# Four loads of v with four consecutive rows per partition, and token order restored as the TensorE transpose is evacuated

## The chip, the cores and the metric

The kernel runs on one core of one Trainium2 chip. The metric is the device time of one execution in microseconds (us). The engines are PE (TensorE, matrix multiply), DVE (VectorE), ACT (ScalarE) and POOL (GpSimd, which here mainly issues DMA transfers). This kernel's matmuls write their tiles to PSUM; "evacuating" a tile is copying it from there to SBUF, where the next operations of the kernel read it. Times printed by the profiler are counted from the start of the span, and the span is 1.7 to 1.9 us shorter than the device time of the same run.

## The reference

```python
# q, k, v: (4, 6208, 256) f32; 256 channels, 6208 tokens
qn = q / (norm(q, axis=tokens) + 1e-6);  kn likewise
a  = softmax(kn^T @ qn / tau)             # 256 x 256 for each batch
x  = v @ a                                # 6208 x 256
x_prev = x shifted down by one token
xk = mu_k * x + (1 - mu_k) * x_prev       # xr likewise, with mu_r
k  = relu(xk @ w_k);  out = sigmoid(xr @ w_r) * (k * k @ w_v)
```

The shift by one token matters here: the kernel keeps x transposed, channels on partitions and tokens along the free dimension, and takes the difference of neighbouring columns. So v, transposed, must stand in token order.

## The kernel before

First come the covariance q^T k of batch 0 and its softmax (0 to 41 us). Then a pipeline over 48 blocks of 512 tokens and one of the 256 left over: v is transposed, x = v a, mix with the previous token, up (w_k), square, down (w_v). Blocks 0 to 3 are transposed by PE, because they are needed soon; the other full blocks by the DMA engines. The parts that the change touches:

```python
P = 128; M = 512; S = 4                      # partitions, tokens per block, M // P

def v_load(i):
    v_bf = p2.tile([P, S, C], BF16, ...)
    nc.gpsimd.dma_start(v_bf, v[b, t*M:(t+1)*M, :].rearrange("(s p) c -> p s c", p=P))

def v_transpose_pe(i, evac):                 # blocks 0 to 3
    vT_ps = ps.tile([P, S, 2, P], BF16, ...)
    for s in range(S):
        for h in range(2):
            nc.tensor.transpose(vT_ps[:, s, h], v_bf[:, s, h*P:(h+1)*P], ident)
    if i == 0:
        return lambda: evac(vT0[:, :, 1:].rearrange("c h (s p) -> c s h p", s=S), vT_ps)
    vT = p2.tile([P, S, 2, P], BF16, ...)
    return lambda: evac(vT, vT_ps)
```

and the places where they are used (cuts marked with dots):

```python
    v_load(1); <load w_k, 512 KB>; ...; v_load(2); <load w_v>; v_load(3); ...
    go = v_transpose_pe(0, nc.vector.tensor_copy)   # block 0: evacuated by DVE
    ...; go(); ...; difference(0); exp()
    v_transpose_pe(1, nc.scalar.copy)()             # block 1: by ACT
    keep_warm(2)                                    # two junk matmuls of 512 columns
    weigh_first(0); weigh_first(1); difference(1)   # a_sb, the weights of the softmax
    ... product(a, ih) ...                          # x of block 0 (x_ps)
    # in the loop over blocks:
            if (i, j) in ((-1, 6), (0, 4)):
                v_transpose_pe(i + 3, nc.vector.tensor_copy)()   # blocks 2 and 3: by DVE
```

## Time and profile before

Three runs gave 511.42 to 511.74 us, median 511.45. The profiled run took 512.12 us, with a span of 510.2.

| Reading | Value | View |
|---|---|---|
| PE, DVE, ACT busy | 95%, 87%, 87% of the span | the page, part 1 |
| PE waits for block 1 of v | 1.5 us, once | waits, by PE |
| PE waits for block 2's copy | 0.8 us, once | waits, by PE |
| Copies 128x1024 PSUM to SBUF | 0.67 to 0.68 us on DVE, 1.01 on ACT | timeline |
| PE clock 39.8 to 43.2 us | 0.50 of the full one | windows |

Two lines of the page, the span and the busy times in us with their share and the number of instructions:

```profile
span 510.2 us, 9336 instructions
...
PE 485.9 (95%) x3441; PEld 331.3 (65%) x3441; DVE 444.0 (87%) x751; ACT 446.3 (87%) x925; POOL 99.9 (20%) x146
```

The waits of PE, who waited for whom, then us in total, times, and the longest:

```profile
PE vT_ps L365 <- DMA v_bf<-in_v_dram: 1.5, 1, 1.5
...
PE xT_ps L386 <- DVE vT L371: 0.8, 1, 0.8
```

The timeline at the places that the argument uses; columns are start, duration, engine, line, operation, output<-input, shapes, and in brackets the idle time before and what ended it:

```profile
38.52 0.67 DVE L368 COPY vT<-vT_ps 128x1024 bf16<-128x1024 bf16 x1
...
40.39 1.04 PE L365 MATMUL vT_ps<-ident,v_bf 128*128 128x128 bf16 x8 [1.50 <-DMA v_bf<-in_v_dram]
...
42.08 0.63 PE L410 MATMUL x_ps<-vT,a_sb 128*128 128x256 bf16 x2
...
48.53 0.69 DVE L469 TENSOR_TENSOR delta<-xT 128x1024 bf16<-128x1024 bf16 x1 [1.11 <-ACT xT L388]
...
52.20 0.68 DVE L371 COPY vT<-vT_ps 128x1024 bf16<-128x1024 bf16 x1
...
52.94 0.59 PE L386 MATMUL xT_ps<-vT,a_sb 128*128 128x512 bf16 x2 [0.83 <-DVE vT L371]
```

The first line is block 0's copy, the second block 1's transposes, waiting for their load. Then come the first matmul of x for block 0, the first "delta" of the loop (the token difference of block 1), block 2's copy, and the x matmul that waits for it. The load of block 1, asked for alone (the line of the load, in the window of that one issue):

```profile
L349 POOL DMA_DIRECT2D v_bf<-in_v_dram x1: 940/940/940, 33.3 to 33.3; - x1
...
DMA to landing us min/median/max: 7.1/7.1/7.1
```

POOL worked 940 ns at it from 33.3 us, and the data had landed 7.1 us after the start, at 40.4. The windows view, of which the columns needed are the stretch, its length, the busy times of PE, PEld, DVE, ACT and POOL, then the granted PE clock, the DMA share and GB/s:

```profile
39.00:40.00 1.00, 0.00 (x0) 0.00 (x0) 0.93 (x6) 1.00 (x5) 0.16 (x1) 0.88 1.13 199
...
41.00:42.00 1.00, 1.00 (x7) 0.53 (x5) 0.05 (x1) 0.53 (x1) 0.46 (x1) 0.50 1.14 213
...
45.00:46.00 1.00, 0.67 (x5) 0.26 (x4) 1.00 (x3) 0.66 (x2) 0.48 (x2) 1.00 1.45 195
```

In the middle one PE runs at half its clock (0.50 granted). The DMA queues then move 2 KB packets (w_k) at 213 GB/s; in the last one they move 512-byte packets at 195 GB/s.

### The profile page before, as it was taken

The numbers are of one execution on the slowest core, as the hardware profiler recorded it, in microseconds if no ns is written. First come the engines' busy times: TensorE is split into PE (matmuls) and PEld (weight loads), VectorE is DVE, ScalarE is ACT, GpSimd is POOL, SyncE is SP. The second block draws the span as 40 slices with busy tenths as digits, with TensorE's granted clock in tenths as the row PEclk, the third lists the DMA queues.
The fourth block names the chain that finished last, engine by engine and source line by source line (L and its number), as shares of the span: only waits on it lengthen the run. The fifth ranks groups of instructions, "written<-read, shape, count | busy, mean of one in ns | idle before, by whom it ended". The sixth has DMA issues, their size and how long they took to land. (4 is left out here: it accounts for less than half of the span.)

```text
span 510.2 us, 9336 instructions
## 1 busy us (share of the span) xinstructions
PE 485.9 (95%) x3441; PEld 331.3 (65%) x3441; DVE 444.0 (87%) x751; ACT 446.3 (87%) x925; POOL 99.9 (20%) x146
## 2 busy tenths in 40 slices
PE   4678999999999999999999999999999999999996
PEld 1345666766567677676666767667666666666675
DVE  3776899999999999999979999999878787878884
ACT  5767999999899999999899999999897888888784
POOL 0044342223054132221243133000131100000000
PEclk9998999999999999999999999999999999999999
DMA  8999999999989999997599999924497763333123
GB/s 330 409 299 201 191 173 199 143 192 199 201 153 198 180 205 172 171 184 134 102 157 227 173 173 177 176 74 116 84 178 137 143 106 97 93 85 83 45 81 104
DMA packets 133462, 83.46 MB, mean 164 GB/s; under 512 B 50660, under 2 KB 126760, under 8 KB 133416
## 3 DMA queue, kind: packets, MB, share of 16 engines
q0 software_dynamic: 56592, 33.01, 50.1%
q1 hardware_dynamic: 76504, 49.59, 41.1%
q8 instruction: 27, 0.44, 0.4%
q10 hardware_dynamic: 320, 0.26, 0.2%
q14 instruction: 19, 0.16, 0.1%
HBM read 78.71 MB, written 25.43 MB: 204 GB/s over the span
## 5 line engine op out<-in xcount | busy, mean ns | idle before, releaser
L499 ACT ACTIVATE kr<-kT_ps 128x512 bf16<-128x512 f32 (+1 forms) x390 | 232.0, 606 | 27.8 <-PE kT_ps L494 24.0
L531 PE MATMUL vr_ps<-w_v_sb,kk 128*128 128x256 bf16 x1536 | 231.0, 273 | 0.1
L494 PE MATMUL kT_ps<-xk,w_k_sb 128*128 128x512 bf16 (+1 forms) x780 | 230.0, 377 | 0.2 <-DVE xk L479 0.2
L531 PEld LDWEIGHTS <-kk 128*128 128x128 bf16 x1536 | 149.5, 98 | 58.9 <-DVE kk L512 1.1
L541 DVE SCALAR_TENSOR_TENSOR res<-res,vr_ps 128x256 f32<-128x256 f32 x192 | 80.1, 417 | 42.8 <-ACT res L540 42.8
L512 DVE TENSOR_TENSOR kk<-kr 128x1536 bf16<-128x1536 bf16 (+2 forms) x148 | 117.1, 791 | 0.2 <-ACT kr L499 0.2
L494 PEld LDWEIGHTS <-w_k_sb 128*128 128x128 bf16 x780 | 75.5, 98 | 27.5 <-issue 0.6
L230 DVE TENSOR_TENSOR acc<-acc,sq 128x1024 f32<-128x1024 f32 x69 | 84.2, 1220 | 0.0
L540 ACT ACTIVATE res<-vr_ps 128x256 f32<-128x256 f32 x192 | 76.5, 398 | 1.3 <-PE vr_ps L531 1.3
L527 PE MATMUL vr_ps<-w_r_sb,xr 128*128 128x256 bf16 x384 | 73.3, 272 | 1.2 <-DVE res L541 1.2
L479 DVE SCALAR_TENSOR_TENSOR xr<-delta,mu_t,xT 128x512 bf16<-128x512 bf16 x94 | 70.1, 746 | 0.0
L479 DVE SCALAR_TENSOR_TENSOR xk<-delta,mu_t,xT 128x512 bf16<-128x512 bf16 x94 | 70.1, 746 | 0.0
L527 PEld LDWEIGHTS <-xr 128*128 128x128 bf16 x384 | 37.6, 98 | 46.4 <-issue 2.6
L388 ACT CAST xT<-xT_ps 128x512 bf16<-128x512 f32 x94 | 55.4, 589 | 12.1 <-PE xT_ps L386 11.9
L386 PE MATMUL xT_ps<-vT,a_sb 128*128 128x512 bf16 x188 | 55.9, 379 | 0.9 <-DVE vT L371 0.8
L242 PE MATMUL s_ps<-qk 128*128 128x256 bf16 (+1 forms) x294 | 55.8, 273 | 0.0
L127 POOL DMA_DIRECT2D qk<-in_q_dram x39 | 26.2, 672 | 136.6 <-ACT kr L499 53.3
L226 ACT ACTIVATE sq<-qk 128x1024 f32<-128x1024 bf16 (+1 forms) x49 | 51.0, 1041 | 0.0
L349 POOL DMA_DIRECT2D v_bf<-in_v_dram x48 | 37.1, 776 | 50.7 <-DMA vT<-v_bf 32.4
L190 PE MATMUL s_ps<-qk 128*128 128x384 bf16 (+2 forms) x98 | 20.3, 352 | 16.0 <-ACT qk L147 14.9
L469 DVE TENSOR_TENSOR delta<-xT 128x1024 bf16<-128x1024 bf16 x47 | 32.3, 686 | 1.1 <-ACT xT L388 1.1
L242 PEld LDWEIGHTS <-qk 128*128 128x128 bf16 (+1 forms) x294 | 28.5, 98 | 5.6 <-issue 0.8
(105 smaller groups left out, 242.1 us busy)
## 6 DMA issues: line engine op xcount, KB each, us to landing
out_dram<-res SPq DMA_DIRECT2D x47, 512.0 KB, 4.2
v_bf<-in_v_dram POOLq DMA_DIRECT2D x48, 256.0 KB, 9.0
qk<-in_q_dram POOLq DMA_DIRECT2D x36, 256.0 KB, 8.0
qk<-in_k_dram POOLq DMA_DIRECT2D x36, 256.0 KB, 8.8
f<-in_q_dram SPq DMA_DIRECT2D x11, 512.0 KB, 9.4
f<-in_k_dram SPq DMA_DIRECT2D x11, 512.0 KB, 9.9
vT<-v_bf SPq DMA_TRANSPOSE x44, 6.7
f<-in_q_dram SPq DMA_DIRECT2D x2, 256.0 KB, 9.0
```

The costliest lines, as they stand in the source:

```text
L230: nc.vector.tensor_tensor(sums[b], sums[b], t, op=OP.add)
L242: nc.tensor.matmul(s_ps[:, ih, :], rows_at(qk, b, g, 0)[:rows, s, ih * P:(ih + 1) * P], rows_at(qk, b, g, 1)[:rows, s, :], start=t0 and ih ...
L386: nc.tensor.matmul(xT_ps, a_sb[:, b, ih, dh * P:(dh + 1) * P], vT[:, :, ih, :], start=ih == 0, stop=ih == 1)
L388: nc.scalar.copy(xT[:, dh, 1:], xT_ps)
L479: nc.vector.scalar_tensor_tensor(o[:, dh], st[i, "d"][:, dh], mu[:, dh:dh + 1], st[i, "x"][:, dh, :M], op0=OP.mult, op1=OP.add)
L494: nc.tensor.matmul(kT_ps[:, :m], w_k_sb[:, dh, fh * P:(fh + 1) * P], xk[:, dh, :m], start=dh == 0, stop=dh == 1)
L499: nc.scalar.activation(kr, kT_ps[:, :m], AF.Relu, scale=0.5 ** 0.5)
L512: nc.vector.tensor_tensor(st[i, "kk"][:, fh // 4 * 4 + lo:fh + 1, :m], kr, kr, op=OP.mult)
L527: nc.tensor.matmul(vr_ps[:, D:], xr[:, dh, s * P:(s + 1) * P], w_r_sb[:, dh, :], start=dh == 0, stop=dh == 1)
L531: nc.tensor.matmul(vr_ps[:, :D], kk[:, fh, s * P:(s + 1) * P], w_v_sb[:, fh, :], start=fh == 0, stop=fh == 7)
L540: nc.scalar.activation(res[:, s], vr_ps[:, D:], AF.Tanh, scale=0.5)
L541: nc.vector.scalar_tensor_tensor(res[:, s], res[:, s], 1.0, vr_ps[:, :D], op0=OP.add, op1=OP.mult)
```

## The change

The intent: a load that gives each partition four consecutive rows reads 128 runs of 4 KB instead of 512 of 1 KB. That is a quarter of the packets (the run with the change has 131,926 for 133,462, so 384 fewer for each of the four loads) and less work on POOL (548 ns for the load of block 1, against 940). The transposed tile then has its tokens out of order, and since the kernel copies it out of PSUM anyway, the copy can put them in order for nothing, if a stepped source costs nothing.

```diff
     def v_load(i):
-        nc.gpsimd.dma_start(v_bf, v[b, t * M:(t + 1) * M, :].rearrange("(s p) c -> p s c", p=P))
+        nc.gpsimd.dma_start(v_bf, v[b, t * M:(t + 1) * M, :].rearrange(
+            "(p s) c -> p s c" if i < S else "(s p) c -> p s c", p=P))
     def v_transpose_pe(i, evac):
         ...
+        src = vT_ps.rearrange("c s h p -> c h p s")
         if i == 0:
-            return lambda: evac(vT0[:, :, 1:].rearrange("c h (s p) -> c s h p", s=S), vT_ps)
-        vT = p2.tile([P, S, 2, P], BF16, name="vT", tag="vT", bufs=5)
-        st[i, "vT"] = vT
-        return lambda: evac(vT, vT_ps)
+            vT = vT0[:, :, 1:]
+        else:
+            vT = p2.tile([P, S, 2, P], BF16, ...).rearrange("c s h p -> c (s h p)")
+            st[i, "vT"] = vT.rearrange("c (h s p) -> c s h p", h=2, s=S)
+            vT = vT.rearrange("c (h m) -> c h m", h=2)
+        return lambda: evac(vT.rearrange("c h (p s) -> c h p s", s=S), src)
```

The copy writes densely; its source now steps 256 elements (512 bytes) from one element to the next, in groups of four. Below, "the new load" is the first part and "the stepped copy" the second.

More of the change, by code (lines that the diff above doesn't have):

```diff
@@ L365, in v_transpose_pe @@
                 nc.tensor.transpose(vT_ps[:, s, h], v_bf[:, s, h * P:(h + 1) * P], ident)
+        src = vT_ps.rearrange("c s h p -> c h p s")
         if i == 0:
-            return lambda: evac(vT0[:, :, 1:].rearrange("c h (s p) -> c s h p", s=S), vT_ps)
-        vT = p2.tile([P, S, 2, P], BF16, name="vT", tag="vT", bufs=5)
-        st[i, "vT"] = vT
-        return lambda: evac(vT, vT_ps)
+            vT = vT0[:, :, 1:]
+        else:
+            vT = p2.tile([P, S, 2, P], BF16, name="vT", tag="vT", bufs=5).rearrange("c s h p -> c (s h p)")
+            st[i, "vT"] = vT.rearrange("c (h s p) -> c s h p", h=2, s=S)
+            vT = vT.rearrange("c (h m) -> c h m", h=2)
+        return lambda: evac(vT.rearrange("c h (p s) -> c h p s", s=S), src)
     def x_half(i, dh):
```

## The prediction

> **What bounds the kernel.** The page shows PE busy 485.9 of 510.2 us (95%), DVE and ACT 87%; the chain that ended last runs through PE matmuls, so after the start a delay of PE is a delay of the end. In the table of windows PE is idle 15 us in 0 to 31 us (the first covariance, fed by DMA) and busy 10.0 of 10 us in 60 to 70. The change touches only 32 to 60 us.
>
> **What changes.** Four of 48 loads of v: same bytes, but 128 runs of 4 KB (f32) instead of 512 of 1 KB. Costs, from the trace:
>
> - Descriptors on POOL: v loads 742 to 940 ns each; the q/k loads of the second batch, already of the new shape, 531 to 591. About 0.25 us less per load.
> - Packets: 512 of 512 B (60 ns each) become 128 of 2 KB (173 ns each). In steady stretches these queues move 195 and 213 GB/s, so a load takes 1.33 and 1.23 us of the queue: 0.1 us saved[...].
> - Evacuation: the source now steps 512 B between neighbouring elements. The DVE copies of 128x1024 take 0.67 to 0.68 us[...]. I expect [...]as the 128x1024 f32 add has (1.22 us): 1.2 us, 0.54 more, for blocks 0, 2 and 3. Block 1's copy is on ACT (1.01 us) and should stay near 1.0.
> - PE work is unchanged; the written tile is dense.
>
> **What is on the critical path.**
>
> 1. Gain. PE waits 1.5 us for v of block 1 (waits by PE: "DMA v_bf", once), until 40.39; the load was issued at 33.3 and landed after 7.1 us[...]. Transposes, two warming matmuls, then the x products (42.08), ACT (43.47) and DVE (43.88) follow. With earlier issue and fewer packets I expect landing at 39.4 to 40.0. DVE then nearly binds: its copy of block 0 (38.52) pushes the softmax weights from 40.71 to about 41.25 and the second difference to 41.6, so products can start near 41.3. Gain 0.4 to 0.9 us, perhaps 1.5 if the half clock (39.8 to 43.2 us, granted 0.5) is avoided.
> 2. Loss. PE waits for block 2's copy (52.20 to 52.88; wait 0.83 us, "DVE vT", until 52.94), and DVE has no gap from 48.5 on. The extra 0.54 us goes straight to PE, which has almost no idle time later.
> 3. Block 3's copy (59.45, used at 62.7) has 2.6 us of slack and DVE idles 0.55 us at 68.3: nearly free.
>
> Sum: about -0.6 + 0.54, near zero.
>
> **Prediction.** 511.3 us, 8 times in 10 between 510.3 and 512.3. Faster by over 2%: 1%; within 2%: 98%; slower by over 2%: 1%.
>
> **What would show each step.** POOL v loads 0 to 3 at 0.55 to 0.6 us; some 1,500 packets fewer; DVE vT copies at 1.2 us, the ACT copy at 1.0; PE's wait for v_bf under 1.5 us, x products before 42.08; from the first product to block 2's x matmul, 10.86 us before, about 11.4; from 60 us on the same schedule, shifted.
>
> **What would make it wrong.** A strided PSUM read [...] (2 us or more): slower by 1 to 3 us. Block 1 landing no earlier, because other traffic[...] sets it: about 512.0. The PE clock staying full around 40 us: about 510. Shifted loads colliding later: some tenths either way.

The terms of its sum, -0.6 for block 1 and +0.54 for block 2's copy, come to -0.06 us from 511.45, and the prediction put its middle at 511.3. The 0.54 is the 1.22 us of the f32 add less 0.68; that a stepped bf16 copy would take as long as that add was the author's estimate, not shown before the run. The landing at 39.4 to 40.0 us is an estimate; of what the text gives for it, POOL's 0.25 us and the queue's 0.1 us remain, so most of the 0.4 to 0.9 us of gain is that estimate.

## The result, and the profile after

Ratios here are the mean time of one kernel's fast runs over that of the other's of the same rounds, so they are not quite the ratios of the medians quoted beside them.

The first measurement: 510.56 us median (510.54 to 510.63, 4 runs), before 511.44 (510.46 to 511.74, 4 runs), ratio 0.9986, 95% interval 0.9969 to 1.0004. That is the same within 2%, and 0.3 us above the lower end of the predicted range, 510.3 to 512.3. The lines of the changed kernel that answer to those shown of before, first the page:

```profile
span 508.8 us, 9277 instructions
...
PE 481.0 (95%) x3382; PEld 330.3 (65%) x3441; DVE 445.2 (88%) x751; ACT 446.1 (88%) x925; POOL 99.2 (20%) x146
```

(The 59 PE records fewer are missing from the trace, not from the program: the weight loads, one for each matmul, are 3441 in both.) The waits of PE:

```profile
PE xT_ps L390 <- DVE vT L375: 1.4, 1, 1.4
...
PE x_ps L414 <- DVE a_sb L328: 0.7, 1, 0.7
```

The timeline at the same places:

```profile
38.32 1.20 DVE L375 COPY vT<-vT_ps 128x1024 bf16<-128x1024 bf16 x1
...
38.38 0.61 PE L366 MATMUL vT_ps<-ident,v_bf 128*128 128x128 bf16 x8
...
39.86 1.01 ACT L375 COPY vT<-vT_ps 128x1024 bf16<-128x1024 bf16 x1
...
40.64 0.39 PE L414 MATMUL x_ps<-vT,a_sb 128*128 128x256 bf16 x2 [0.69 <-DVE a_sb L328]
...
46.59 0.69 DVE L473 TENSOR_TENSOR delta<-xT 128x1024 bf16<-128x1024 bf16 x1 [1.11 <-ACT xT L392]
...
50.26 1.22 DVE L375 COPY vT<-vT_ps 128x1024 bf16<-128x1024 bf16 x1
...
51.53 0.59 PE L390 MATMUL xT_ps<-vT,a_sb 128*128 128x512 bf16 x2 [1.36 <-DVE vT L375]
```

The load of block 1, asked for alone, landed at 33.1 + 5.2 = 38.3 us:

```profile
L349 POOL DMA_DIRECT2D v_bf<-in_v_dram x1: 548/548/548, 33.1 to 33.1; - x1
...
DMA to landing us min/median/max: 5.2/5.2/5.2
```

The window from 41 to 42 us of the changed kernel, now at full clock:

```profile
41.00:42.00 1.00, 1.00 (x12) 0.80 (x10) 0.44 (x3) 0.47 (x2) 0.01 (x1) 1.00 1.17 219
```

These two traces tell a neat story. The load landed at 38.3 instead of 40.4 us. The x products started 1.44 us earlier (40.64 against 42.08), now held by DVE's weights. The half clock was gone, and the first delta came 1.94 us earlier (46.59 against 48.53). The stepped copy of block 2 took 0.54 us longer, and PE waited 1.36 instead of 0.83 us for it, so 1.41 us were left at the x matmul (51.53 against 52.94) and at the end (508.8 against 510.2). The experiments show that the last third of this story is right, and that most of the first two thirds is what these two executions happened to draw.

### The profile page after: what moved, and what is told of

It reads as the page before. It is cut to its first block, busy times and chain, and to the rows that moved or that the text cites. A ratio compares the mean times of both kernels' runs of the same rounds, so it can differ in the third digit from the quotient of the medians.

```text
span 508.8 us, 9277 instructions
## 1 busy us (share of the span) xinstructions
PE 481.0 (95%) x3382; PEld 330.3 (65%) x3441; DVE 445.2 (88%) x751; ACT 446.1 (88%) x925; POOL 99.2 (20%) x146
## 2 busy tenths in 40 slices
DMA packets 131926, 83.46 MB, mean 164 GB/s; under 512 B 50660, under 2 KB 124712, under 8 KB 131880
## 5 line engine op out<-in xcount | busy, mean ns | idle before, releaser
L498 PE MATMUL kT_ps<-xk,w_k_sb 128*128 128x512 bf16 (+1 forms) x722 | 217.6, 377 | 0.3 <-DVE xk L483 0.2
L349 POOL DMA_DIRECT2D v_bf<-in_v_dram x48 | 36.0, 752 | 48.6 <-DMA vT<-v_bf 29.0
## 6 DMA issues: line engine op xcount, KB each, us to landing
out_dram<-res SPq DMA_DIRECT2D x47, 512.0 KB, 4.0
f<-in_q_dram SPq DMA_DIRECT2D x11, 512.0 KB, 9.4
f<-in_k_dram SPq DMA_DIRECT2D x11, 512.0 KB, 9.9
```

What stands on the lines that cost most here:

```text
L498: nc.tensor.matmul(kT_ps[:, :m], w_k_sb[:, dh, fh * P:(fh + 1) * P], xk[:, dh, :m], start=dh == 0, stop=dh == 1)
```

## The experiments

Each kernel was run with a profile and in five rounds, beside the kernel before. The theory (A): the new load lets block 1 land earlier, which starts the whole pipeline earlier; block 2's stepped copy lies on the path and costs about 0.5 us; block 0's costs little and block 3's nothing. Rival B: all four new loads give their share, through fewer packets and less POOL work. A second question grew from the runs: is the half clock around 40 us a property of the kernel before? The edits are shown shortened; the files of most runs name the blocks in two lists, one for the new load and one for the stepped copy.

### Blocks 0 and 1 only

```diff
-            "(p s) c -> p s c" if i < S else "(s p) c -> p s c", p=P))
+            "(p s) c -> p s c" if i < 2 else "(s p) c -> p s c", p=P))
 # and the stepped copy for blocks 0 and 1 alone
```

> Only blocks 0 and 1 are loaded and evacuated the new way; blocks 2 and 3 as before. Theory A (the gain is block 1 landing earlier plus the full PE clock; the loss is block 2's slower DVE copy on PE's path): same schedule as the whole change up to block 2's copy, which goes back to 0.68 us, so 0.5 us faster than the change: 510.0 us. Rival B (every one of the four loads gives its share of the gain, by fewer packets and shorter descriptor work): slower than the change, 510.9 to 511.2.

Measured: 510.76 us median (510.03 to 512.0, 6 runs), ratio 0.9999 (0.9979 to 1.0018). The spread of 2 us is larger than what was to be told apart, and the eleven runs of the kernel before beside it spread as far (509.6 to 512.05). By their times these runs decide nothing between A and B; what they showed is that a single pair of traces decides nothing about the start either.

### Block 1 only

The same edit with block 1 alone, whose copy is on ACT.

> Only block 1 the new way, whose copy is on ACT, so all DVE copies are 0.68 us as before. Theory A: block 1 lands about 1 us earlier than before (39.3), DVE has the softmax weights 0.5 us earlier than with the whole change, products start at 40.3 to 40.8, block 2's copy costs nothing: 509.8 to 510.5 us. Rival B: about a quarter of the gain, 511.2.

Measured: 510.17 us median, but one run of 514.62 (ratio 1.0, 0.9971 to 1.0029). Four of the five others, 509.9 to 510.2, are where A expected them, the fifth is at 511.0. The profile fell on the slow one. Its start is as predicted (products at 40.46), and the time was lost elsewhere, at 115 us, where PE waited once for a DMA transpose of a later block (waits, by PE):

```profile
PE xT_ps L398 <- DMA vT<-v_bf: 2.9, 1, 2.9
```

No other trace used here shows that wait.

### Blocks 2 and 3 only

> Only blocks 2 and 3 the new way. Theory A: nothing gained, block 2's copy adds 0.53 us on PE's path and block 3's next to nothing: 0.4 to 0.7 us slower than the kernel before. Rival B: as fast as before or faster.

Measured: 511.0 us median (510.11 to 512.47, 6 runs), ratio 1.0008 (0.9988 to 1.0028). The times lean to A without deciding. The trace decides on the copy: the two DVE copies take 1.22 us, and PE's wait for block 2 is that of the change (waits, by PE):

```profile
PE xT_ps L398 <- DVE vT L378: 1.4, 1, 1.4
```

This kernel loads blocks 0 and 1 as before, and yet its block 1 had landed at 39.2 us, its products started at 40.27 and there was no half clock. So the kernel before can have that early start too.

### The new load alone (wrong result)

All four loads new, evacuated without reordering, so that the tokens of four blocks are out of order (relative error 0.40).

```diff
+    "(p s) c -> p s c" if i < S else "(s p) c -> p s c"      # the load
     return lambda: evac(vT, vT_ps)                           # the copy as before
```

> All four loads the new way, evacuated as before without reordering: the result is wrong on purpose (tokens of the first four blocks out of order). Theory A: the whole gain without the loss of block 2 (0.53) and without block 0's longer copy ahead of the softmax weights (up to 0.53): 509.4 to 510.0 us. If the copies cost nothing on PE's path it equals the change: 510.5.

Measured: 509.78 us median (509.38 to 510.96, 6 runs), ratio 0.9981 (0.9963 to 0.9999). This half of the change gains about 1.0 us, with an interval from near 0 to 1.9.

### The stepped copy alone (wrong result)

Loads as before, all four copies stepped (relative error 0.39).

> Loads as before, evacuated with the stepped source: the result is wrong on purpose. Theory A: products still wait for block 1 until 40.4 us, so block 0's longer copy is free, block 1's ACT copy stays at 1.0 us, block 2's costs 0.53 and block 3's about nothing: 0.4 to 0.7 us slower than before, at equal PE clock. If blocks 0 and 3 are on the path too, 1.0 to 1.6 us slower.

Measured: five runs of 510.79 to 513.99 us, ratio 1.0022 (1.0001 to 1.0043). This half loses about 1.1 us, with an interval from 0.05 to 2.2 that holds both expectations. Part of the 1.1 us is the one run of 513.99, which has no trace to explain it; without it the mean is 511.63, about 0.75 above the kernel before. The profiled run is not used: it took 2903 us, with matmuls of 128x256 at a mean of 1044 ns instead of 273. The views print a clock of 1.00 for it, so what slowed it is not shown.

### Junk matmuls ahead of block 1's transposes

```diff
+    keep_warm(6)
     v_transpose_pe(1, nc.scalar.copy)()
     keep_warm(2)
```

> The kernel before, with six more junk matmuls of 512 columns ahead of block 1's transposes, to fill PE's wait for block 1; nothing of the loads changed. If the half clock around 40 us is its own part of the gain: no half clock, products start near 41.4 and take 0.5 us less, 0.6 to 1.2 us faster than before although block 1 lands no earlier. If the landing alone makes the gain: as before within 0.2 us.

Measured: 511.49 us median (510.19 to 514.49, 6 runs), ratio 1.0016 (0.9992 to 1.0041). A miss. The half clock was not prevented, and the junk itself ran under it and held up transposes whose data had been there since 39.3 us. The timeline of PE in this run:

```profile
39.35 2.77 PE L603 MATMUL junk_ps<-fill,ones 128*128 128x512 bf16 x6
41.91 0.92 PE L368 MATMUL vT_ps<-ident,v_bf 128*128 128x128 bf16 x8
```

The window from 39 to 40 us of the same run, with a granted clock of 0.57 on average:

```profile
39.00:40.00 1.00, 1.00 (x6) 0.60 (x5) 0.97 (x4) 0.81 (x4) 0.28 (x2) 0.57 1.07 184
```

Five traces have a half-clock spell near 40 us. In the kernel before it lasts 3.41 us by the record of the granted clock (39.76 to 43.18 us). In the runs with blocks 0 and 1, with junk first and with block 1 late, the mean clocks of the 1 us windows give 3.40 to 3.42 us; of the spell in the changed kernel's second trace only the start was read. Its place differs from run to run: it begins at 39.76, 39.16, 39.14, 41.96 and 40.22 us, in the order named. In the run with junk first (0.57 on average from 39 to 40 us is 0.86 us at 0.50) it began before the junk at 39.35, so the junk came too late to prevent it. What brings such a spell on, and whether earlier junk would prevent it, is not shown.

### Block 1 loaded later

The whole change, with the 512 KB load of w_k issued ahead of block 1.

```diff
-    v_load(1)
     nc.gpsimd.dma_start(w_k_sb, moe_w_k.rearrange("(ko ki) f -> ki ko f", ki=P))
+    v_load(1)
```

> The whole change, with block 1's load issued behind the 512 KB load of w_k, so that it lands some 1.5 to 2.5 us later (about 40 to 40.8 us) with the same new shape of all four loads. Theory A: the gain is gone, products start at 42 or later and block 2's copy still costs 0.5: 0.3 to 1.5 us slower than before. Rival B: most of the gain stays, 510.6 to 511.0.

Measured: 514.65 us median (514.51 to 515.67, 5 runs), ratio 1.008 (1.0064 to 1.0097). The direction is A's and the size is a miss: block 1 came not at 40 to 40.8 but at 42.6 us (waits, by PE).

```profile
PE vT_ps L368 <- DMA v_bf<-in_v_dram: 4.0, 1, 4.0
```

The timeline of the same run:

```profile
42.60 1.04 PE L368 MATMUL vT_ps<-ident,v_bf 128*128 128x128 bf16 x8 [4.01 <-DMA v_bf<-in_v_dram]
...
44.28 0.63 PE L422 MATMUL x_ps<-vT,a_sb 128*128 128x256 bf16 x2
...
50.73 0.69 DVE L481 TENSOR_TENSOR delta<-xT 128x1024 bf16<-128x1024 bf16 x1 [1.11 <-ACT xT L400]
```

The first delta was 4.14 us after that of the changed kernel, and the span 4.1 us longer. The first trace of the kernel before is the better comparison, since there too PE waited for block 1 and had the half clock afterwards: against it block 1 came 2.21 us later (42.60 against 40.39), the products 2.20 and the first delta 2.20. So once block 1 is the last to come, its landing moves the rest one for one. B, which let most of the gain stay, falls with its number, though a delay this large would hide a share of some tenths.

### Two rows per partition

```diff
+  nc.gpsimd.dma_start(v_bf.rearrange("p (a s) c -> p a s c", a=2),
+                      v[b, t*M:(t+1)*M, :].rearrange("(a p s) c -> p a s c", a=2, p=P))   # blocks 0 to 3
 # the copies step in the same way
```

> Two consecutive rows per partition in each of two halves instead of four: packets of 1 KB, 256 per load; copies stepped as in the change. If block 1's earlier landing comes from larger packets: it lands between the two kernels (39.0 to 39.8 us), copies at 1.2 us, time 510.4 to 511.2. If it comes from the shorter descriptor work or chance: it lands where its descriptor time puts it, near 38.3 to 38.6 or at 40.3.

Measured: 511.15 us median (510.79 to 511.52, 5 runs), ratio 1.0004 (0.999 to 1.0018). Block 1 landed at 33.5 + 5.2 = 38.7 us, earlier than the range expected for it, although POOL worked at this load as long as in some runs with the old load (753 ns in the run with junk first). The load's own line:

```profile
L350 POOL DMA_DIRECT2D v_bf<-in_v_dram x1: 792/792/792, 33.5 to 33.5; - x1
...
DMA to landing us min/median/max: 5.2/5.2/5.2
```

So less work on POOL is not what an early landing needs. That the size of the packets sets it is not shown by this run, since the landing did not fall between the two.

### The change once more, and the kernel before once more

> The whole change once more, for its spread. The runs so far fit one sum: the span is the start of the first delta on DVE (the first full block's difference) plus 461.6 us, or plus 462.15 where block 2's copy is stepped. If landings and the clock vary from run to run in it as in its parts, the times spread over 510.2 to 512 and the mean lies within 0.4 us of the kernel before. If the change really removes the half clock, all runs lie at 510.5 to 510.7 again and none has a mean clock of 0.997 or less.

> The kernel before against itself: the ratio should be 1.000 within 0.002, times 509.6 to 512.1, about four in ten runs with a mean clock of 0.997 or less. Its second profile shows whether block 1's landing at 40.4 us was typical (again 40 to 40.8) or late by chance (39.0 to 39.5, as in the runs whose first two loads were unchanged).

Measured for the change: 510.85 us median (510.25 to 512.61, 6 runs), ratio 1.001 (0.9993 to 1.0027), two of six runs with a mean clock of 0.997 or less. Measured for the kernel before against itself: 510.26 us median (509.7 to 511.18, 6 runs), ratio 0.9993 (0.9979 to 1.0007). The second pair of traces tells the opposite story to the first. The timeline of the changed kernel, with a span of 510.8 us:

```profile
38.91 0.62 PE L366 MATMUL vT_ps<-ident,v_bf 128*128 128x128 bf16 x8 [1.58 <-DMA v_bf<-in_v_dram]
...
39.57 1.23 DVE L375 COPY vT<-vT_ps 128x1024 bf16<-128x1024 bf16 x1 [1.34 <-PE vT_ps L366]
...
41.91 0.61 PE L414 MATMUL x_ps<-vT,a_sb 128*128 128x256 bf16 x2 [0.43 <-DVE a_sb L328]
...
48.65 0.69 DVE L473 TENSOR_TENSOR delta<-xT 128x1024 bf16<-128x1024 bf16 x1 [1.11 <-ACT xT L392]
...
52.32 1.22 DVE L375 COPY vT<-vT_ps 128x1024 bf16<-128x1024 bf16 x1
```

and that of the kernel before, with a span of 507.8 us:

```profile
39.43 0.62 PE L365 MATMUL vT_ps<-ident,v_bf 128*128 128x128 bf16 x8 [0.74 <-DMA v_bf<-in_v_dram]
...
40.32 0.38 PE L410 MATMUL x_ps<-vT,a_sb 128*128 128x256 bf16 x2
...
46.25 0.69 DVE L469 TENSOR_TENSOR delta<-xT 128x1024 bf16<-128x1024 bf16 x1 [1.11 <-ACT xT L388]
...
49.92 0.68 DVE L371 COPY vT<-vT_ps 128x1024 bf16<-128x1024 bf16 x1
...
50.66 0.59 PE L386 MATMUL xT_ps<-vT,a_sb 128*128 128x512 bf16 x2 [0.83 <-DVE vT L371]
```

Now it is the changed kernel that waits, 1.58 us, and for block 0; it is the one with the half clock (from 40.2 us), and its first delta is 2.4 us later than that of the kernel before.

### What all traces have in common

| Kernel of the trace | Block 2's copy | First delta | Span | Span minus first delta |
|---|---|---|---|---|
| before | 0.68, DVE | 48.53 | 510.2 | 461.7 |
| before, again | 0.68, DVE | 46.25 | 507.8 | 461.6 |
| blocks 0 and 1 | 0.69, DVE | 47.66 | 509.3 | 461.6 |
| new load alone | 0.68, DVE | 46.38 | 507.9 | 461.5 |
| junk first | 0.68, DVE | 49.01 | 510.6 | 461.6 |
| changed | 1.22, DVE | 46.59 | 508.8 | 462.2 |
| changed, again | 1.22, DVE | 48.65 | 510.8 | 462.2 |
| blocks 2 and 3 | 1.22, DVE | 46.21 | 508.3 | 462.1 |
| block 1 late | 1.22, DVE | 50.73 | 512.9 | 462.2 |
| two rows | 1.22, DVE | 46.97 | 509.1 | 462.1 |
| blocks 1 and 2 on ACT | 1.01, ACT | 46.23 | 507.6 | 461.4 |
| the same, again | 1.01, ACT | 46.20 | 507.7 | 461.5 |

(The trace of block 1 alone, with its lost time at 115 us, is left out: 46.40 and 512.8.) The table splits each run into a start, whose length varies by over 2 us from run to run in the same kernel, and a rest that repeats within 0.2 us. In the rest the stepped copy of block 2 costs 462.1 - 461.6 = about 0.5 us, in every trace. Block 3's stepped copy costs nothing that can be seen: the run with blocks 2 and 3 alone and the second trace of before have their first delta together (46.21 and 46.25), the second is 0.50 us apart (55.52 and 55.02), and after block 3's copy the third is still 0.50 apart (66.83 and 66.33). In the start, the earliest delta with a dense copy of block 0 is at 46.2 us, in four traces; with a stepped one it is at 46.59. So block 0's stepped copy costs about 0.4 us (46.59 - 46.2) when nothing else is late, an estimate from the best trace of each kind.

### Blocks 1 and 2 only, both evacuated by ACT

ACT takes 1.01 us for the copy with a dense source and 1.01 with a stepped one. So the stepped copies belong on ACT, and with blocks 1 and 2 there DVE is left with no slow copy.

```diff
+    new load and stepped copy for i in (1, 2) only
-                v_transpose_pe(i + 3, nc.vector.tensor_copy)()
+                v_transpose_pe(i + 3, nc.scalar.copy if i < 0 else nc.vector.tensor_copy)()
```

> Blocks 1 and 2 loaded the new way and both evacuated by ACT (1.01 us, stepped or not); blocks 0 and 3 as before. Theory: block 2's copy no longer sits in DVE's unbroken stretch, PE's wait for it (0.8 us before, 1.4 with the change) shrinks to 0.3 or less, and the span is the first delta's start plus 460.8 to 461.2 instead of 461.6: 509.3 to 510.2 us, 0.6 to 1.4 us faster than before. If the wait for block 2's copy was not on the path, no faster than the run with block 1 alone (510.2).

Measured: 509.64 us median (509.41 to 510.23, 6 runs), ratio 0.9981 (0.9967 to 0.9994). The time is as expected, and the sum only in part: PE no longer waits for block 2's copy, but span minus first delta is 461.4, not 460.8 to 461.2. The copy now sits in ACT's stream, as the timeline of this run shows:

```profile
48.27 1.01 ACT L378 COPY vT<-vT_ps 128x1024 bf16<-128x1024 bf16 x1
...
49.16 1.28 ACT L511 ACTIVATE kr<-kT_ps 128x512 bf16<-128x512 f32 x2
...
49.65 0.59 PE L398 MATMUL xT_ps<-vT,a_sb 128*128 128x512 bf16 x2
```

The window from 50 to 60 us of the same run, where the fourth busy time is ACT's:

```profile
50.00:60.00 10.00, 9.78 (x74) 6.84 (x73) 7.42 (x12) 9.97 (x23) 3.96 (x7) 1.00 1.27 202
```

The x matmul runs at 49.65, 1.0 us before that of the second trace of before (50.66, with the first delta at the same place). The next delta, first in this run and then in the second trace of before, is only 0.19 us earlier:

```profile
54.83 0.68 DVE L481 TENSOR_TENSOR delta<-xT 128x1024 bf16<-128x1024 bf16 x1
...
55.02 0.69 DVE L469 TENSOR_TENSOR delta<-xT 128x1024 bf16<-128x1024 bf16 x1
```

From 50 us on ACT is busy 9.97 of 10 us (9.90 in the second trace of before), and a copy put on ACT is paid for there. So ACT binds together with PE in this stretch, and of the 1.0 us some 0.1 to 0.2 are left.

Because this version was picked as the best of several, it was run again, on another chip:

> The version with blocks 1 and 2 loaded the new way and evacuated by ACT, once more, because it was picked as the best of several. If it is truly faster than the kernel before: mean 509.4 to 510.2 us, 0.5 to 1.3 us under the kernel before of the same rounds. If it only drew an early landing and a full clock: within 0.4 us of the kernel before.

Measured: 509.67 us median (509.39 to 510.46, 6 runs), ratio 0.9986 (0.9969 to 1.0003). Over both, 12 runs have a mean of 509.73, beside 510.74 for the 50 runs of the kernel before in these experiments: 1.0 us, or 0.2%, faster. The repeat alone, which was not picked, gives 0.7 us by its ratio, with an interval that just reaches no gain. It has the best mean of the kernels with a correct result.

### All runs together

| Kernel | Fast runs | Mean us | Lowest, highest | Runs with a mean clock of 0.997 or less |
|---|---|---|---|---|
| before | 50 | 510.74 | 509.50, 512.77 | 18, mean 511.48 |
| changed | 10 | 510.99 | 510.25, 512.61 | 2, mean 512.45 |
| blocks 1 and 2 on ACT | 12 | 509.73 | 509.39, 510.46 | 2, mean 510.35 |

The changed kernel is 0.25 us above the kernel before, with a standard error of 0.28 (from the spread of 0.8 us of each over 50 and 10 runs). The four runs of the kernel before in the first measurement are not in the table. The last column serves to count half clocks: one spell of 3.41 us at half clock takes 0.0033 off the mean over 510 us. Where the spell lay is known only for runs with a trace; in that of block 1 alone the page shows it between 115 and 128 us, not at 40. The 18 runs of the kernel before with a mean clock of 0.997 or less had a mean time 1.2 us above the other 32 (511.48 against 510.32), late landings included.

## Why the prediction was right

The time, 510.56 us, lay in the range, and "within 2%" was right. The kernel before alone spreads wider (509.5 to 512.77) than the range of 2 us, so the number by itself says little of the mechanism, and that it fell inside is in part luck. Point by point:

- **What bounds the kernel.** Right: the end moves with PE's x matmul of block 2, and with block 1's landing when that is late (2.20 us for 2.21). Incomplete: after 50 us ACT binds as well, which the prediction did not say; the run with the copy on ACT showed it.
- **Cost of the copies.** Right: 1.20 to 1.23 us on DVE for 1.2 predicted, 1.01 on ACT for 1.0. On DVE the bf16 source of unit step took 0.67 to 0.69 us and the stepped one 1.20 to 1.23, close to the 1.22 of the f32 add that the prediction went by.
- **Loss at block 2, 0.54 us on the path.** Right. It is the 0.5 us of the table, in five traces against five with a dense DVE copy. The check that the prediction named for it, from the first product to block 2's x matmul 10.86 us before and about 11.4 after, missed: it was 10.89 after (40.64 to 51.53), because the 10.86 held the half clock. The second trace of before, without it, has 10.34 (40.32 to 50.66), and against that the change adds 0.55.
- **Block 3 nearly free.** Right, by the same table.
- **Work saved.** Right: 1,536 packets fewer (133,462 to 131,926), and POOL at 548 to 587 ns for loads 1 to 3 of the changed kernel (0.55 to 0.6 predicted), but 680 for load 0.
- **Gain from block 1, 0.4 to 0.9 us.** Right in direction; its size was hard to measure, and whether the packets or POOL's shorter work bring it is not shown. With the old load block 1 landed at 40.4, 39.4, 39.2 and 39.3 us in four traces, mean 39.6. With the new one it landed at 38.3, 39.5, 39.0, 38.8, 39.0, 38.9 and 38.5 in seven, mean 38.9; without the first trace's 40.4 the old mean is 39.3. Counted from its issue, this load landed after 6.0 to 7.1 us in the four traces and after 5.2 to 6.4 in the seven. In the first trace the last packets before it landed come singly, one every 41 ns, from 39.04 to 39.99 us; the trace's list of packets does not name the engine that moved them. The new load alone gained 1.0 us (near 0 to 1.9). What the prediction missed is that block 0 stands in front of it: in three of the four traces with a new load of block 0 and block 1 in its place, PE waited for block 0 instead (0.5, 0.6 and 1.6 us), which landed at 36.1 to 38.8 us, no earlier on average than the 37.2 to 38.0 of the old load.
- **The steps that failed.** First, "until 40.39", one reading of one trace, was taken for the kernel's schedule; its second trace had 39.43. Second, the half clock was treated as something of the kernel before that the change might avoid. By the mean clock it came in 18 of 50 runs before and 2 of 10 after, and these numbers are too few to tell the two apart. Third, "products can start near 41.3" made DVE's weights bind too late: in the first trace they let the products start at 40.64, since block 0's copy began 0.2 us earlier than before and the first product started after the first half of the weights (written from 40.23 us), not after the second (from 40.69).

The sum of the prediction, about -0.6 + 0.54, has the signs that the halves show: the new load alone about -1.0, the stepped copy alone about +1.1, both together +0.25 with a standard error of 0.28. So the change moved the time little because its two halves cancel. Both intervals only just leave out zero, so the sizes of the halves are not confirmed; the traces confirm the 0.5 us at block 2. The prediction counted block 0's slower copy inside its gain, and -1.0 with the 0.4 us of that copy would be its -0.6, but that the numbers agree so closely is in part luck. Open stays whether the small remainder is above zero, what makes one and the same load of block 0 land up to 2.7 us apart from run to run (36.1 and 38.8 in the changed kernel), and whether the new load makes the half clock any rarer.

## What to carry to other kernels

A reordering hidden in a copy was free here on ACT, whose copy took 1.01 us with a dense source and with the stepped one, and not on DVE, whose copy went from 0.67 to 0.69 us to 1.20 to 1.23 and stood where PE waited for it. Then check whether the engine that takes the copy has room: on ACT, busy 9.97 of 10 us, the x matmul of block 2 came 1.0 us earlier and the next delta only 0.19. And before explaining half a microsecond by two traces, profile the same kernel twice: here one kernel's two traces differed by 2.4 us, and splitting the span at one event made the steady part repeat within 0.2 us, so that the 0.5 us could be seen.
